# A side bank for transposes, hashes and sums, two banks for the down product, and preparing steps between the gated groups

## The chip, the core and the metric

The kernel runs on one core of one Trainium2 chip. The metric is the device time of one execution in microseconds (us). The program uses TensorE (PE) for matmuls, VectorE (DVE), ScalarE (ACT), GpSimd (POOL) and SyncE (SP); the last two issue the DMAs. Matmul results land in PSUM, which has eight banks per partition.

## The reference

Two blocks follow each other. The first is an attention whose mask lets a query see only the keys with the same 6-bit hash; the second is a gated feed-forward block on its output.

```python
q_bits = (np.einsum('bhsd,dk->bhsk', q, proj) > 0)     # k_bits alike, 6 bits
mask = q_bucket[:, :, :, None] == k_bucket[:, :, None, :]
scores = np.where(mask, scale * np.matmul(q, k.transpose(0, 1, 3, 2)), -1000000000.0)
attn = np.exp(scores - np.max(scores, axis=-1, keepdims=True))
attn = attn / (np.sum(attn, axis=-1, keepdims=True) + 1e-09)
x = np.matmul(attn, v)        # (4, 8, 768, 64) -> tokens (3072, 512)
g = x @ w_gate                # (512, 1536)
out = (g * (1.0 / (1.0 + np.exp(-g))) * (x @ w_val)) @ w_out
```

All data are float32; the weights come as float64 and are narrowed on the chip.

## The kernel before

The work is cut into 16 pairs of heads (4 batches of 4 pairs), each pair into two halves of 384 queries, each half into 6 chunks of 128 keys. One chunk of one half of one pair is a unit; there are 192.

- `score(u)` makes the scores of a unit for both heads of the pair: a bfloat16 matmul of the hash bits, which puts unequal hashes far below, then the float32 matmul of q and k, into one of two double banks `sc`; ScalarE takes the exponential into a ring of four tiles `A`.
- `attend(u)` multiplies `A` with v into the bank `av`, and VectorE adds `A` to the accumulator `acc`. After the sixth chunk ScalarE copies `av` out.
- `norm(u)` sums `acc` over the partitions with a matmul with ones (`sum`). VectorE adds a small number, takes the reciprocal and writes the normalised half to `xT`.
- `front(n)` prepares a pair in eight steps: four transposes of q or k (`tps`, three 128x128 blocks each; ScalarE copies the result), then four hash matmuls (`hps`, followed on VectorE by a comparison that writes the bits `qb` or `kb`). The steps are run two per two units, while the pair before is worked on.
- `push_ffn(b)` gives 72 atoms for a finished batch: 48 groups of eight matmul instructions (`g` and `val`, alternately; ScalarE's Tanh and VectorE's product free their banks), then 24 parts of the down product, of which four in a row fill one tile `po`; ScalarE copies it to `o` and SP stores it.
- `narrow()` turns the float64 words of the weights into float32 on VectorE, seven operations for each of 36 pieces. The pieces come over POOL's DMA queue.

A float32 matmul of the program is two matmul instructions in the profile. All engines run their own program in the order in which this code issues it. Nothing reorders it, so the order of calls in the loops at the end decides. The first batch has no atoms beside it ("alone"): there the loop takes one unit at a time: score, one step, attend of the unit before, one or two operations of `narrow`. From the second batch on (the gated part) it takes two units at a time: attend of the two units before, score of two units, two steps, then 3.1 atoms on average. When the units are used up, the atoms of the last batch follow by themselves.

PSUM: `sc` two double banks, `av` one, `po` one, and two banks `mm` that transposes, hashes, sums, gate and value groups share in turn. An instruction that wants a bank waits until the reader of its last content has ended.

Of the kernel before, what the change touches and what calls it, by code (L numbers as in the profile page):

```python
# [8 lines left out]
FP32 = mybir.dt.float32  # L9
BF16 = mybir.dt.bfloat16  # L10
I32 = mybir.dt.int32
ALU = mybir.AluOpType
AF = mybir.ActivationFunctionType
# [4 lines left out]
def kernel(  # L18
# [43 lines left out]
    wraw = ctx.enter_context(tc.tile_pool(name="wraw", bufs=2))  # L62
    sc_ps = ctx.enter_context(tc.tile_pool(name="sc_ps", bufs=2, space=PSUM))
    av_ps = ctx.enter_context(tc.tile_pool(name="av_ps", bufs=1, space=PSUM))
    po_ps = ctx.enter_context(tc.tile_pool(name="po_ps", bufs=1, space=PSUM))
    mm_ps = ctx.enter_context(tc.tile_pool(name="mm_ps", bufs=2, space=PSUM))

    ctx.enter_context(tc.manual_schedule())

    def bank(name):  # L70
        return mm_ps.tile([P, 512], FP32, tag="mm", name=name)


    pairs = [(b, pr) for b in range(B) for pr in range(NP)]
# [2 lines left out]
    def load(n):  # L77
        b, pr = pairs[n]
        for name, src in (("q", q), ("k", k)):
            t = raw.tile([P, NCH, 2, D], FP32, tag=name + "raw", name=name + "raw")  # L80
            for h in range(2):
                nc.sync.dma_start(t[:, :, h, :],
                                  src[b, 2 * pr + h].rearrange("(p c) d -> p c d", c=NCH))
            raws[name, n] = t
        t = raw.tile([P, 2, NCH, D], FP32, tag="vraw", name="vraw")
        nc.sync.dma_start(
            t.rearrange("p h c d -> p h (c d)"),
            v[b, 2 * pr : 2 * pr + 2].rearrange("h (p c) d -> p h (c d)", c=NCH),
        )
        raws["v", n] = t  # L90
# [11 lines left out]
            for at in (0, NBITS) if name == "q" else (0,):  # L102
                nc.sync.dma_start(hash_w[name][o : o + D, o + at : o + at + NBITS], proj[:, :])

    def column(name, first, second):
        t = konst.tile([P, 1], FP32, tag=name, name=name)
        nc.vector.memset(t, 0.0)
        for o in (0, D):
            nc.vector.memset(t[o : o + 2 * NBITS], second)
            nc.vector.memset(t[o : o + NBITS], first)  # L110
        return t

    less_q = column("less_q", 0.5, 0.0)
    above_k = column("above_k", 0.0, -1.0)
    times_k = column("times_k", 2.0 * OFF, -OFF)
    ident = konst.tile([P, P], FP32, tag="ident", name="ident")
    make_identity(nc, ident)
    ones = konst.tile([P, D], FP32, tag="ones", name="ones")
# [61 lines left out]
    def narrow_on(n):  # L180
        for _ in range(n):
            next(narrowing, None)
# [5 lines left out]
    T = {}  # L188
    bits = {}

    def front(n):


        def transpose(name, half):
            if half == 0:
                T[name, n] = opnd.tile([P, S], FP32, tag=name + "T", name=name + "T")
                bits[name, n] = opnd.tile([P, S], BF16, tag=name + "b", name=name + "b")
            ps = bank("tps")
            for i in range(CH):
                nc.tensor.transpose(ps[:, i * P : (i + 1) * P],  # L200
                                    raws[name, n][:, half * CH + i, :, :].rearrange("p h d -> p (h d)"),
                                    ident)
            nc.scalar.copy(T[name, n][:, half * HQ : (half + 1) * HQ], ps[:, 0:HQ])

        def hash_bits(name, half):
            cols = slice(half * HQ, (half + 1) * HQ)
            ps = bank("hps")
            nc.tensor.matmul(ps[:, 0:HQ], hash_w[name], T[name, n][:, cols], start=True, stop=True)  # L208
            o = bits[name, n][:, cols]
            if name == "q":  # L210
                nc.vector.tensor_scalar(o, ps[:, 0:HQ], scalar1=0.0, scalar2=less_q,  # L211
                                        op0=ALU.is_gt, op1=ALU.subtract)
            else:
                nc.vector.tensor_scalar(o, ps[:, 0:HQ], scalar1=above_k, scalar2=times_k,
                                        op0=ALU.is_gt, op1=ALU.mult)

        steps = []
        for half in range(2):
            for name in "qk":
                steps.append(lambda name=name, half=half: transpose(name, half))  # L220
        for half in range(2):
            for name in "qk":
                steps.append(lambda name=name, half=half: hash_bits(name, half))
        return steps
# [19 lines left out]
    def attend(u):  # L244
        n, half, c = units[u]
        a = ring[u % RING]
        if c == 0:
            av[n, half] = av_ps.tile([P, 512], FP32, tag="av", name="av")
        ps = av[n, half]
        for h in range(2):  # L250
            nc.tensor.matmul(ps[h * D : (h + 1) * D, 0:AW], raws["v", n][:, h, c, :], a[:, h, :],  # L251
                             start=c == 0, stop=c == NCH - 1)
        if c == 1:
            acc[n, half] = att.tile([P, 2, HQ], FP32, tag="acc", name="acc")
            nc.vector.tensor_tensor(acc[n, half], ring[(u - 1) % RING][:, :, 0:HQ],  # L255
                                    a[:, :, 0:HQ], op=ALU.add)
        elif c > 1:
            nc.vector.tensor_tensor(acc[n, half], acc[n, half], a[:, :, 0:HQ], op=ALU.add)  # L258
        if c == NCH - 1:
            av[n, half] = att.tile([P, AW], FP32, tag="avs", name="avs", bufs=1)  # L260
            nc.scalar.copy(av[n, half], ps[:, 0:AW])  # L261

    def norm(u):
        n, half, _ = units[u]
        b, pr = pairs[n]
        if pr == 0 and half == 0:
            xT[b] = xp.tile([P, NP, S], FP32, tag="xT", name="xT")
        ps = bank("sum")
        t = acc.pop((n, half))
        for h in range(2):  # L270
            nc.tensor.matmul(ps[h * D : (h + 1) * D, 0:HQ], ones, t[:, h, :], start=True, stop=True)  # L271
        a = av.pop((n, half))
        r = att.tile([P, HQ], FP32, tag="r", name="r", bufs=1)
        nc.vector.tensor_scalar(r, ps[:, 0:HQ], scalar1=S * EPS, scalar2=None, op0=ALU.add)  # L274
        nc.vector.reciprocal(r, r)  # L275
        e = att.tile([P, 1], FP32, tag="e", name="e")
        nc.vector.tensor_scalar(e, a[:, HQ : HQ + 1], scalar1=EPS, scalar2=None, op0=ALU.mult)
        nc.vector.scalar_tensor_tensor(out=xT[b][:, pr, half * HQ : (half + 1) * HQ],  # L278
                                       in0=a[:, 0:HQ], scalar=e, in1=r,
                                       op0=ALU.add, op1=ALU.mult)  # L280
        if pr == NP - 1 and half == 1:
            push_ffn(b)
# [4 lines left out]
    def push_ffn(b):  # L287
# [22 lines left out]

        def down(half, i, fs):
            if fs[0] == 0:
                now["o"] = po_ps.tile([P, DM], FP32, tag="po", name="po")
            ps = now["o"]
            for f in fs:
                nc.tensor.matmul(ps, hs[half][f][:, i * P : (i + 1) * P], wo[:, f, :],  # L316
                                 start=f == 0, stop=f == NF - 1)
            if fs[-1] == NF - 1:
                o = ffn.tile([P, DM], FP32, tag="o", name="o")
                nc.scalar.copy(o, ps)  # L320
                rows = out[b * S : (b + 1) * S, :].rearrange("(p c) m -> p c m", c=NCH)
                nc.sync.dma_start(rows[:, half * CH + i, :], o)
# [10 lines left out]

    for step in front(0):
        step()
    N = len(units)
    per = 2 * NCH
    steps = []  # L340
    due = []

    def prepare(u):
        n, at = divmod(u, per)
        if at == 0 and n + 1 < len(pairs):
            steps.extend(front(n + 1))
        if at == per - 2 and n + 2 < len(pairs):
            load(n + 2)

    def finish(u):  # L350
        while due:
            norm(due.pop(0))
        attend(u)
        if units[u][2] == NCH - 1:
            due.append(u)

    alone = NP * per
    for u in range(alone):
        prepare(u)
        score(u)  # L360
        if u % per >= 2 and steps:
            steps.pop(0)()
        if u > 0:
            finish(u - 1)
        narrow_on(2 if u % 6 == 3 else 1)

    rate = 3.1
    credit = 0.0
    left = [alone - 1]
    for u in range(alone, N + 2, 2):  # L370
        while left:
            finish(left.pop(0))
        if u >= N:
            while due:
                norm(due.pop(0))
            break
        prepare(u)
        score(u)
        score(u + 1)
        left = [u, u + 1]  # L380
        for _ in range(2):
            if u % per >= 2 and steps:
                steps.pop(0)()
        credit = credit + rate if atoms else 0.0
        while atoms and credit >= 1.0:
            credit -= 1.0
            atoms.pop(0)()
            narrow_on(4)
    for atom in atoms:
        atom()  # L390

# [31 lines left out]
```

## Time and profile before

| | |
|---|---|
| median of 3 runs | 1227.14 us (1227.07 to 1228.08) |
| profiled execution | 1227.17 us |
| its span | 1225.4 us |
| granted clock, mean | 0.997 |
| PE busy | 1174.4 us (96%) |
| VectorE busy | 540.5 us (44%) |
| ScalarE busy | 257.7 us (21%) |
| first score, first gate group | 13.50 us, 131.84 us |

PE is the engine that is nearly always busy, but a matmul's end in the profile is modelled, so that successive matmuls overlap a little. What one thing costs is read from the distance of two starts. In the first 340 us VectorE is busy too, since it narrows the weights there.

### The profile page before, as it was taken

Reading aid. Unit: us, or ns where it says so; the run is one execution under the profiler, and the core shown is the slowest. Engines: PE = TensorE matmul, PEld = TensorE weight load, DVE = VectorE, ACT = ScalarE, POOL = GpSimd, SP = SyncE. Lnnn points to the kernel's source line nnn. Section 1 sums busy time; section 2 is a strip of 40 time slices with the busy share of each in tenths; the row PEclk is TensorE's granted clock in tenths of the full one; section 3 lists DMA queues with packets and bytes.
Section 4 is the critical chain, followed back from the end, with each engine's and each line's share of the span. In section 5 each row is a group of like instructions: output and inputs, shape, how many; then the busy total and the mean of one; then the engine's idle time right before and its main releaser. Section 6 shows DMA issues by size and latency. Waiting matters only on the chain.

```text
span 1225.4 us, 10930 instructions
## 1 busy us (share of the span) xinstructions
PE 1174.4 (96%) x4480; PEld 569.4 (46%) x4480; DVE 540.5 (44%) x814; ACT 257.7 (21%) x409; POOL 19.3 (2%) x44
## 2 busy tenths in 40 slices
PE   8999989989899999999999999999999999999998
PEld 3333445445444444545553444554544334555533
DVE  4999788888832324234440333434234222222100
ACT  3444212212112122121221213222121111000000
POOL 0000000000000000000000000000000000000000
PEclk9999999999999999999999999999999999999999
DMA  6222314223200110100002012010000000000000
GB/s 155 74 74 74 91 52 124 68 70 108 69 22 18 43 48 1 39 1 1 13 1 56 18 34 48 1 39 1 14 1 1 18 18 17 1 1 0 1 26 26
DMA packets 63698, 44.76 MB, mean 37 GB/s; under 512 B 51872, under 2 KB 55968, under 8 KB 63648
## 3 DMA queue, kind: packets, MB, share of 16 engines
q1 hardware_dynamic: 58752, 26.23, 8.3%
q0 software_dynamic: 4896, 17.83, 4.6%
q8 instruction: 35, 0.57, 0.2%
q14 instruction: 15, 0.12, 0.0%
HBM read 37.76 MB, written 6.29 MB: 36 GB/s over the span
## 4 chain that ended last, share of the span: by engine, by line
PE 82%; DVE 12%; ACT 4%; issue 1%; DMA 0%; SPq 0%; ACTq 0%
PE po L316 21%; PE g L295 20%; PE val L295 19%; PE sc L240 9%; PE av L251 8%; DVE r L275 3%; ACT A L242 2%; DVE acc L258 2%; PE hps L208 2%; PE sum L271 2%; PE tps L200 1%; DVE qb L211 1%; DVE acc L255 1%; ACT o L320 1%; DVE xT L278 1%
## 5 line engine op out<-in xcount | busy, mean ns | idle before, releaser
L295 PE MATMUL val<-xT,wv 128*128 128x384 f32 x768 | 266.0, 489 | 15.9 <-DVE qb L211 10.9
L295 PE MATMUL g<-xT,wg 128*128 128x384 f32 x768 | 268.4, 493 | 12.5 <-DVE qb L211 7.8
L316 PE MATMUL po<-wo,ht 128*128 128x512 f32 x576 | 256.9, 597 | 9.8 <-ACT o L320 9.8
L242 ACT ACTIVATE A<-sc 128x768 f32<-128x768 f32 x192 | 155.6, 812 | 283.3 <-PE sc L240 256.8
L295 PEld LDWEIGHTS val<-xT,wv 128*128 128x128 f32 x768 | 144.2, 190 | 122.6 <-DVE qb L211 16.7
L295 PEld LDWEIGHTS g<-xT,wg 128*128 128x128 f32 x768 | 145.1, 191 | 119.7 <-DVE qb L211 12.9
L316 PEld LDWEIGHTS po<-wo,ht 128*128 128x128 f32 x576 | 106.7, 190 | 149.8 <-issue 126.4
L240 PE MATMUL sc<-qT,kT 64*128 64x384 f32 x768 | 155.1, 482 | 0.0
L258 DVE TENSOR_TENSOR acc<-acc,A 128x768 f32<-128x768 f32 x128 | 122.2, 954 | 66.8 <-ACT A L242 63.5
L302 DVE SCALAR_TENSOR_TENSOR t<-t,g 128x384 f32<-128x384 f32 x96 | 53.1, 554 | 222.9 <-ACT t L301 222.8
L251 PE MATMUL av<-A,vraw 128*64 128x386 f32 x768 | 149.4, 499 | 0.3 <-ACT A L242 0.2
L301 ACT ACTIVATE t<-g 128x384 f32<-128x384 f32 x96 | 47.0, 490 | 437.3 <-PE g L295 425.4
L307 DVE SCALAR_TENSOR_TENSOR ht<-t,val 128x384 f32<-128x384 f32 x96 | 53.1, 553 | 142.2 <-PE val L295 142.2
L251 PEld LDWEIGHTS av<-A,vraw 128*64 128x64 f32 x768 | 47.2, 136 | 83.9 <-issue 82.7
L275 DVE RECIPROCAL r<-r 128x384 f32<-128x384 f32 x32 | 81.7, 2553 | 1.1
L240 PEld LDWEIGHTS sc<-qT,kT 64*128 64x128 f32 x768 | 68.9, 189 | 16.4 <-issue 16.4
L274 DVE TENSOR_SCALAR r<-sum 128x384 f32<-128x384 f32 x32 | 17.7, 554 | 123.4 <-PE sum L271 122.9
L240 PE MATMUL sc<-qb,kb 64*128 64x384 bf16 x384 | 63.8, 329 | 0.0
L240 PEld LDWEIGHTS <-kb 64*128 64x128 bf16 x384 | 18.5, 93 | 81.2 <-issue 70.9
L320 ACT COPY o<-po 128x512 f32<-128x512 f32 x24 | 14.0, 585 | 155.4 <-PE po L316 148.4
L211 DVE TENSOR_SCALAR qb<-hps,less_q 128x384 bf16<-128x384 f32 x32 | 19.6, 614 | 45.0 <-PE hps L208 45.0
L261 ACT COPY avs<-av 128x386 f32<-128x386 f32 x32 | 15.4, 482 | 82.3 <-PE av L251 82.3
(56 smaller groups left out, 443.4 us busy)
## 6 DMA issues: line engine op xcount, KB each, us to landing
qraw<-in_q_dram SPq DMA_DIRECT2D x32, 192.0 KB, 4.4
kraw<-in_k_dram SPq DMA_DIRECT2D x32, 192.0 KB, 5.1
vraw<-in_v_dram SPq DMA_DIRECT2D x16, 384.0 KB, 3.5
words<-in_moe_w_val_dram POOLq DMA_DIRECT2D x12, 512.0 KB, 3.8
words<-in_moe_w_out_dram POOLq DMA_DIRECT2D x12, 512.0 KB, 3.6
out_dram<-o SPq DMA_DIRECT2D x24, 256.0 KB, 2.0
words<-in_moe_w_gate_dram POOLq DMA_DIRECT2D x10, 512.0 KB, 3.9
words<-in_moe_w_gate_dram SPq DMA_DIRECT2D x2, 512.0 KB, 6.1
```

The source lines that it names most:

```text
L211: nc.vector.tensor_scalar(o, ps[:, 0:HQ], scalar1=0.0, scalar2=less_q, op0=ALU.is_gt, op1=ALU.subtract)
L240: nc.tensor.matmul(sc[:, h, 0:HQ], x["k", n][rows, ks], x["q", n][rows, qs], start=start, stop=not start)
L242: nc.scalar.activation(ring[u % RING][:, :, 0:HQ], sc[:, :, 0:HQ], AF.Exp, scale=SCALE)
L251: nc.tensor.matmul(ps[h * D : (h + 1) * D, 0:AW], raws["v", n][:, h, c, :], a[:, h, :], start=c == 0, stop=c == NCH - 1)
L258: nc.vector.tensor_tensor(acc[n, half], acc[n, half], a[:, :, 0:HQ], op=ALU.add)
L275: nc.vector.reciprocal(r, r)
L295: nc.tensor.matmul(ps[:, 0:HQ], w[:, j, f * P : (f + 1) * P], x[:, j, half * HQ : (half + 1) * HQ], start=j == 0, stop=j == NJ - 1)
L301: nc.scalar.activation(t, ps[:, 0:HQ], AF.Tanh, scale=0.5)
L302: nc.vector.scalar_tensor_tensor(out=t, in0=t, scalar=1.0, in1=ps[:, 0:HQ], op0=ALU.add, op1=ALU.mult)
L307: nc.vector.scalar_tensor_tensor(out=ht, in0=now["t"], scalar=0.5, in1=ps[:, 0:HQ], op0=ALU.mult, op1=ALU.mult)
L316: nc.tensor.matmul(ps, hs[half][f][:, i * P : (i + 1) * P], wo[:, f, :], start=f == 0, stop=f == NF - 1)
L320: nc.scalar.copy(o, ps)
```

## The change

- Transposes, hashes and sums leave the two banks `mm` and get one bank of their own (`side_bank`), the one that the down product had. Only the first pair's steps, ahead of the loop, still use `mm`.
- The down product takes its tiles from the two banks `mm` in turn.
- The first batch is worked on two units at a time too, by the same loop as the rest.
- In an iteration the scores of two units now come first, then the sum that is due, then the attends of the two units before, then the atoms; the two steps are run after the first and the second atom. Without atoms, they run one right after the other, followed by two or three operations of `narrow`.
- The bits of q are made by ScalarE as a sign (Sign with a bias column), and the columns for k change their scale to match.
- VectorE's addition ahead of the reciprocal goes: the small number is added in the first addition of `acc`, and the reciprocal reads PSUM itself.

The diff, cut to its core:

```diff
+    aux_ps = ctx.enter_context(tc.tile_pool(name="aux_ps", bufs=1, space=PSUM))
...
+    def side_bank(name):
+        return aux_ps.tile([P, 512], FP32, tag="aux", name=name)
...
-    def front(n):
+    def front(n, bank=side_bank):
...
             if name == "q":
-                nc.vector.tensor_scalar(o, ps[:, 0:HQ], scalar1=0.0, scalar2=less_q,
-                                        op0=ALU.is_gt, op1=ALU.subtract)
+                nc.scalar.activation(o, ps[:, 0:HQ], AF.Sign, bias=nudge)
...
-            nc.vector.tensor_tensor(acc[n, half], ring[(u - 1) % RING][:, :, 0:HQ],
-                                    a[:, :, 0:HQ], op=ALU.add)
+            nc.vector.scalar_tensor_tensor(out=acc[n, half], in0=ring[(u - 1) % RING][:, :, 0:HQ],
+                                           scalar=S * EPS / P, in1=a[:, :, 0:HQ],
+                                           op0=ALU.add, op1=ALU.add)
...
-        ps = bank("sum")
+        ps = side_bank("sum")
...
-        nc.vector.tensor_scalar(r, ps[:, 0:HQ], scalar1=S * EPS, scalar2=None, op0=ALU.add)
-        nc.vector.reciprocal(r, r)
+        nc.vector.reciprocal(r, ps[:, 0:HQ])
...
-                now["o"] = po_ps.tile([P, DM], FP32, tag="po", name="po")
+                now["o"] = bank("po")
...
+    for u in range(0, N + 2, 2):
         n, at = divmod(u, per)
+        if u < N:
+            if at == 0 and n + 1 < len(pairs):
+                steps.extend(front(n + 1))
+            if at == per - 2 and n + 2 < len(pairs):
+                load(n + 2)
+            score(u)
+            score(u + 1)
         while due:
             norm(due.pop(0))
+        for x in left:
+            attend(x)
+            if units[x][2] == NCH - 1:
+                due.append(x)
         left = [u, u + 1]
+        mine = [steps.pop(0) for _ in range(2) if u % per >= 2 and steps]
+        if not atoms:
+            credit = 0.0
+            for step in mine:
+                step()
+            narrow_on(3 if u % 12 == 6 else 2)
+            continue
+        credit += rate
         while atoms and credit >= 1.0:
             credit -= 1.0
             atoms.pop(0)()
             narrow_on(4)
+            if mine:
+                mine.pop(0)()
```

Three places show what this does to the order on the engines. `tps<-ident,qraw` is a transpose of q, `hps<-qT,hashq` the hash matmul of q, `sc` a score, `av` an attend, `sum` the sum.

PE in the first batch, at the end of the first half of a pair, before:

```order
L240 MATMUL sc<-qT,kT 128x384 x2
L208 MATMUL hps<-kT,hashk 128x384
L271 MATMUL sum<-acc,ones 64x384 x2
L251 MATMUL av<-A,vraw 64x386 x2
L240 LDWEIGHTS kb
L240 MATMUL sc<-qb,kb 128x384
L240 LDWEIGHTS kb
L240 MATMUL sc<-qb,kb 128x384
L240 MATMUL sc<-qT,kT 128x384 x2
L208 MATMUL hps<-qT,hashq 128x384
```

and after:

```order
L244 MATMUL sc<-qT,kT 128x384 x2
L276 MATMUL sum<-acc,ones 64x384 x2
L255 MATMUL av<-A,vraw 64x386 x4
L213 MATMUL hps<-qT,hashq 128x384
L213 MATMUL hps<-kT,hashk 128x384
L244 LDWEIGHTS kb
```

Between the sum and the next hash there was an attend and a whole unit of scores; now two attends stand there, and the two hashes follow each other.

PE in a gated iteration with hashes, before:

```order
L240 MATMUL sc<-qT,kT 128x384 x2
L208 MATMUL hps<-qT,hashq 128x384
L208 MATMUL hps<-kT,hashk 128x384
L295 MATMUL val<-xT,wv 128x384 x4
L295 MATMUL g<-xT,wg 128x384 x4
L295 MATMUL val<-xT,wv 128x384 x4
L251 MATMUL av<-A,vraw 64x386 x4
```

and after:

```order
L244 MATMUL sc<-qT,kT 128x384 x2
L276 MATMUL sum<-acc,ones 64x384 x2
L255 MATMUL av<-A,vraw 64x386 x4
L299 MATMUL val<-xT,wv 128x384 x4
L213 MATMUL hps<-qT,hashq 128x384
L299 MATMUL g<-xT,wg 128x384 x4
L213 MATMUL hps<-kT,hashk 128x384
L299 MATMUL val<-xT,wv 128x384 x4
```

The hashes stood in a row ahead of the groups; now each has a group ahead of it and one behind it, and the attends stand behind the scores.

VectorE at a sum of the first batch, before:

```order
L214 TENSOR_SCALAR kb<-hps,above_k,times_k 128x384
L274 TENSOR_SCALAR r<-sum 128x384
L275 RECIPROCAL r<-r 128x384
L277 TENSOR_SCALAR e<-avs 128x1
L278 SCALAR_TENSOR_TENSOR xT<-avs,e,r 128x384
L160 SCALAR_TENSOR_TENSOR wg<-words,wg 128x512
L211 TENSOR_SCALAR qb<-hps,less_q 128x384
```

and after:

```order
L279 RECIPROCAL r<-sum 128x384
L281 TENSOR_SCALAR e<-avs 128x1
L282 SCALAR_TENSOR_TENSOR xT<-avs,e,r 128x384
L259 SCALAR_TENSOR_TENSOR acc<-A 128x768
L218 TENSOR_SCALAR kb<-hps,above_k,times_k 128x384
```

The bank of the sum was free after the short addition; now the reciprocal is its reader. The comparison for q is gone from this queue.

## Rows read from the trace of the kernel before

**Rows 1.** Page, part 1: busy time and share of the span, instructions.

```profile
PE 1174.4 (96%) x4480; PEld 569.4 (46%) x4480; DVE 540.5 (44%) x814; ACT 257.7 (21%) x409; POOL 19.3 (2%) x44
```

**Rows 2.** PE's waits over the run: who for whom; us in total, times, longest us.

```profile
PE val L295 <- DVE qb L211: 10.9, 6, 3.4
PE po L316 <- ACT o L320: 9.8, 14, 0.7
PE g L295 <- DVE qb L211: 7.8, 5, 3.5
...
PE val L295 <- ACT qT L203: 4.8, 9, 0.5
PE g L295 <- ACT qT L203: 4.5, 9, 0.5
```

**Rows 3.** Timeline, gated transposes in two stretches: start us, us, engine, line, operation, count, [idle].

```profile
457.81 1.52 PE L251 MATMUL av<-A,vraw 128*64 128x386 f32 x8
...
459.26 0.34 PE L240 MATMUL sc<-qb,kb 64*128 64x384 bf16 x2
...
460.98 0.55 PE L200 MATMUL tps<-ident,qraw 128*128 128x128 f32 x3
...
461.37 0.49 PE L200 MATMUL tps<-ident,kraw 128*128 128x128 f32 x3
...
461.87 0.47 ACT L203 COPY qT<-tps 128x384 f32<-128x384 f32 x1
...
462.40 2.85 PE L295 MATMUL val<-xT,wv 128*128 128x384 f32 x8 [0.54 <-ACT qT L203]
...
371.81 0.49 PE L200 MATMUL tps<-ident,kraw 128*128 128x128 f32 x3
372.14 2.74 PE L316 MATMUL po<-wo,ht 128*128 128x512 f32 x6
```

**Rows 4.** Timeline, two hash matmuls in a gated iteration.

```profile
486.88 0.91 PE L208 MATMUL hps<-qT,hashq 128*128 128x384 f32 x2
...
487.63 0.81 PE L208 MATMUL hps<-kT,hashk 128*128 128x384 f32 x2
```

**Rows 5.** Timeline, two long waits; then windows: busy us by engine, PEclk, DMA share.

```profile
253.36 2.85 PE L295 MATMUL val<-xT,wv 128*128 128x384 f32 x8 [3.40 <-DVE qb L211]
...
334.76 5.49 PE L295 MATMUL g<-xT,wg 128*128 128x384 f32 x8 [3.52 <-DVE qb L211]
...
250.00:300.00 50.00, 46.11 (x180) 24.66 (x182) 44.00 (x76) 9.03 (x15) 3.79 (x7) 1.00 0.29 88
300.00:350.00 50.00, 44.50 (x170) 22.22 (x167) 37.85 (x64) 9.68 (x15) 2.21 (x4) 0.93 0.15 53
```

**Rows 6.** Timeline, two tiles of the last down product.

```profile
1199.94 10.57 PE L316 MATMUL po<-wo,ht 128*128 128x512 f32 x24 [0.72 <-ACT o L320]
...
1211.23 10.57 PE L316 MATMUL po<-wo,ht 128*128 128x512 f32 x24 [0.72 <-ACT o L320]
```

**Rows 7.** Chain that ended last: start us, us, what; a down tile nobody stops.

```profile
640.66 10.30 PE po L316 x24
```

**Rows 8.** Page, part 5: costliest groups.

```profile
L301 ACT ACTIVATE t<-g 128x384 f32<-128x384 f32 x96 | 47.0, 490 | 437.3 <-PE g L295 425.4
...
L211 DVE TENSOR_SCALAR qb<-hps,less_q 128x384 bf16<-128x384 f32 x32 | 19.6, 614 | 45.0 <-PE hps L208 45.0
```

**Rows 9.** Timeline, first batch: first score, two sums, a reciprocal, first gate group.

```profile
13.50 0.34 PE L240 MATMUL sc<-qb,kb 64*128 64x384 bf16 x2
...
42.77 0.87 PE L271 MATMUL sum<-acc,ones 128*64 128x384 f32 x4 [0.77 <-DVE acc L258]
...
44.27 2.55 DVE L275 RECIPROCAL r<-r 128x384 f32<-128x384 f32 x1
...
70.74 0.87 PE L271 MATMUL sum<-acc,ones 128*64 128x384 f32 x4 [0.78 <-DVE acc L258]
...
131.84 2.85 PE L295 MATMUL g<-xT,wg 128*128 128x384 f32 x8 [0.48 <-ACT qT L203]
```

More of the change, by code (lines that the diff above doesn't have):

```diff
@@ L64 @@
     av_ps = ctx.enter_context(tc.tile_pool(name="av_ps", bufs=1, space=PSUM))
-    po_ps = ctx.enter_context(tc.tile_pool(name="po_ps", bufs=1, space=PSUM))
+    aux_ps = ctx.enter_context(tc.tile_pool(name="aux_ps", bufs=1, space=PSUM))
     mm_ps = ctx.enter_context(tc.tile_pool(name="mm_ps", bufs=2, space=PSUM))
@@ L103, with column @@
                 nc.sync.dma_start(hash_w[name][o : o + D, o + at : o + at + NBITS], proj[:, :])
-    def column(name, first, second):
+    def column(name, first, second, third, rest):
         t = konst.tile([P, 1], FP32, tag=name, name=name)
-        nc.vector.memset(t, 0.0)
+        nc.vector.memset(t, rest)
         for o in (0, D):
+            nc.vector.memset(t[o : o + 2 * NBITS + 1], third)
             nc.vector.memset(t[o : o + 2 * NBITS], second)
@@ L111, in column @@
         return t
-    less_q = column("less_q", 0.5, 0.0)
-    above_k = column("above_k", 0.0, -1.0)
-    times_k = column("times_k", 2.0 * OFF, -OFF)
+    nudge = column("nudge", -1e-37, -1e-37, 1.0, -1e-37)
+    above_k = column("above_k", 0.0, -1.0, -1.0, 0.0)
+    times_k = column("times_k", OFF, -OFF / 2, -NBITS * OFF / 2, 0.0)
     ident = konst.tile([P, P], FP32, tag="ident", name="ident")
@@ L331, in push_ffn @@
                     atoms.append(lambda half=half, i=i, f=f: down(half, i, range(f, f + 3)))
-    for step in front(0):
+    for step in front(0, bank):
         step()
@@ L339 @@
     per = 2 * NCH
+    rate = 3.1
+    credit = 0.0
     steps = []
+    left = []
     due = []
-    def prepare(u):
+    for u in range(0, N + 2, 2):
         n, at = divmod(u, per)
[L345 to L350, printed above, removed]
+        if u < N:
[5 more added lines that the diff above has]
+            score(u + 1)
         while due:
             norm(due.pop(0))
[L353 to L379, printed above, removed]
-        left = [u, u + 1]
[L381 to L384, printed above, removed]
+        for x in left:
+            attend(x)
+            if units[x][2] == NCH - 1:
+                due.append(x)
+        left = [u, u + 1]
+        mine = [steps.pop(0) for _ in range(2) if u % per >= 2 and steps]
+        if not atoms:
+            credit = 0.0
+            for step in mine:
[3 more added lines that the diff above has]
+        credit += rate
         while atoms and credit >= 1.0:
@@ L388 @@
             narrow_on(4)
+            if mine:
+                mine.pop(0)()
+        for step in mine:
+            step()
+    while due:
+        norm(due.pop(0))
     for atom in atoms:
```

## The prediction

> **What bounds the kernel now.** I read the page's busy shares first: PE is busy 1174.4 of 1225.4 us [rows 1], so a gain is either less PE work or less waiting. The matmuls stay the same in number and shape; what can go is waiting and changes of order. Then the waits of PE [rows 2]: five lines hold 37.8 us, of three kinds. PE waits for a bank that VectorE frees after a hash (7.8 + 10.9 us, 11 times), for a bank that ScalarE frees after a transpose (4.5 + 4.8 us, 18 times), for the one bank of the down product (9.8 us, 14 times). Then the timeline around one wait of each kind, because "idle" counts from a modelled end: the spacing of starts is the whole cost.
>
> **Down product, two banks: -13.3 us.** A tile of 24 matmuls takes 10.30 us when nothing stops it [rows 7]; where it must wait for the copy, the next tile starts 11.29 us after it (1199.94 to 1211.23 [rows 6]). That is 0.99 us; some waits stand beside a change of array shape that costs up to 0.1 anyway, so I take 0.95, 14 times [rows 2]. With two banks in turn, the copy has a whole tile's time. The gate and value groups share these two banks, but a batch's down product begins only after its last value group. Nothing new is late here.
>
> **Steps between gated groups: -12.6 and -23.1 us.** Before, two transposes run back to back and the next gate or value group needs the bank that the first has filled: the second transpose starts at 461.37 and the group at 462.40, 1.03 us, where a transpose of the same shape that nobody holds up needs 0.33 (371.81 to 372.14) [rows 3]. 0.7 us, 18 times: 12.6. For hashes the same wait is for VectorE: 18.7 us of idle in 11 waits [rows 2], and in each the drain that the modelled end adds, 0.16 us (a transpose's 0.49 less its 0.33 [rows 3]): 20.5. In one place more was lost: after a 3.52 us wait a gate group took 5.49 us in place of 2.85, in a stretch whose granted clock was 0.93 [rows 5]: 2.6. After the change a step lies behind a group and ahead of another, on its own bank, and the next step comes one group (2.6 us or more) later. Its copy or Sign takes about 0.5 us [rows 3, 8], so the bank is free by then. The Sign is not in the trace: lower bound the 0.47 us copy of the same shape, upper the 0.61 of the VectorE form it replaces; I take 0.49, the Tanh's mean, the nearest in engine and shape [rows 8]. 32 of them, 16 us more on an engine busy 257.7 us [rows 1], nothing on the path. The program has one table load before and after.
>
> The sum's bank is now held until the reciprocal ends. In a gated iteration: sum starts 1.73 us after the first score (two scores take 1.72 [rows 3]), ends 0.87 later, reciprocal 2.55 [rows 9]: free at about 5.2. Two attends and one group end at 1.73 + 0.70 + 1.45 + 2.68 = 6.55, and only then does a step want the bank. 1.3 us of slack, so no wait, unless VectorE starts the reciprocal late. That can happen where the weights are narrowed: VectorE is busy 44.0 of 50 us there [rows 5]. It loses 32 hash comparisons (0.61 us each [rows 8]) and 32 additions ahead of the reciprocal; the first addition of each accumulator gets a third operand (I estimate from nothing up to 0.3 us, 32 times). I count 1 us for this stretch; the bounds are 0 and all that hashes cost today, 23.
>
> Sequence changes on PE: before, an iteration goes groups, attends, scores, steps; now groups, scores, attends. There are three changes of array shape in both. The one that the rows show costs 0.06 us at the first transpose (0.39 against 0.33 [rows 3]), the others I estimate at up to three times that; I take the balance as 0, within 2 us either way.
>
> **First batch in twos, one side bank: +10.7 us.** This stretch has no groups between steps, and I work it out by itself. Before, one pair of heads takes 27.97 us (sum to sum, 42.77 to 70.74), with a 0.77 us wait at each of these two sums [rows 9]. After, a pair is six iterations of two scores and two attends, 3.17 us bare (457.81 to 460.98 [rows 3]). Two have no step: 3.17 each. The four others issue two steps with nothing between and a single bank:
> - two transposes: 0.1 for the extra change of shape, then from the first to the second 0.55 modelled, 0.05 to ScalarE, 0.47 copy, 0.06 back [rows 3] = 1.13, then 0.4 for the second: 4.8.
> - two hashes: 3.17 + 0.1, then 0.91 [rows 4] + 0.05 + 0.49 + 0.06 = 1.5, then 0.85: 5.6.
> - transposes in the iteration with a sum: they wait for the reciprocal, 1.73 + 0.87 + 2.55 + 0.1 = 5.25, then 1.13 + 0.43: 6.8.
> - hashes in the iteration with the other sum: 5.25 + 1.5 + 0.85: 7.6.
>
> Together 2 x 3.17 + 4.8 + 5.6 + 6.8 + 7.6 = 31.1, so 3.2 more per pair, though the twos have halved the changes of shape and the sum no longer waits. The first pair has no early sum and starts with scores only: 31.1 - 2.0 - 1.3 = 27.8. From the first score (13.50 [rows 9]) to the first gate group: 27.8 + 3 x 31.1 + 3.17 + 3.87 = 128.1, so 141.6 to 141.9, against 131.84 [rows 9]: +10. By then before has done two transposes that now follow: +0.65. What is queued behind these waits is PE's whole stream; ScalarE's and VectorE's exponentials and additions just come later. VectorE loses two additions and two comparisons per pair here, and PE waited for it only at sums. SP's reload of v waits for attends up to one unit later, a whole pair before it is needed. Narrowing is 54 operations done instead of 56 when the first group is issued, and the first value group follows 4 more: enough. Bounds: if both waits were hidden, the stretch would gain 12 us (16 x 0.83 + 7 x 1.4 = 23 less); if every copy and reciprocal also stood behind a 0.81 us exponential, 16 x 0.8 = 13 us worse.
>
> **The sum.** 1225.4 - 13.3 - 12.6 - 23.1 + 10.7 + 1 = 1188.1 us of span; 1.8 us lie around it (1227.17 less 1225.4), and the profiled execution agrees with the median of 1227.14. **1190 us.**
>
> **Rivals.**
> (a) The first batch loses nothing: the side bank comes free sooner, because the reciprocal reads a bank as soon as the first half of a sum is in, or the copies are quicker. Against it: both steps need one bank and the copies and the reciprocal have their rows. Half of the 23 us hidden gives about 1179.
> (b) The hash waits come back as waits for VectorE elsewhere, on the gate and value banks or through a late reciprocal, in the stretch where it narrows. For it: 44.0 of 50 us busy. Against: each group frees its bank half a microsecond after VectorE reaches it, and PE needs it a group later. All of the 23.1: 1213; half: 1201.
> (c) Slower than before: the first batch falls to half clock. Its waits, 1.4 and 0.8 us in each iteration of some 6, could make TensorE look idle; its roughly 95 us of matmuls would double, to about 1285. The whole gain of 37 us is gone once 37 us of matmul work runs at 1.2 GHz. Against: a wait of 3.40 us left the granted clock at 1.00 [rows 5], and only the 3.52 us one was followed by a slow group.
> The Trainium skill ("TensorE: Matmul & The Clock Gate", section "A second HAM failure mode: psum-queue depth-cycling") says that short idles of PE between groups of matmuls that cycle through PSUM banks can make the clock swing between its two levels. By that rule (c) would hold; no run here has shown it after waits of 1.4 us.
> (d) That it doesn't do what it says: the down product has two banks to itself, so at least 13.3 us are nearly sure; for no change all else would have to cancel.
>
> **How the numbers follow.** The forecast has 0.68, (a) 0.15, (b) 0.12, (c) 0.03, no change 0.02. The forecast's own spread is 1183 to 1197. The range reaches half into (a) and to the middle of (b), 1176 to 1206; outside lie about 0.05 of (a), 0.06 of (b), (c), (d) and a few hundredths of the forecast. This kernel's measurement can tell 0.2% from no change, 2.5 us. Faster 0.95, same 0.02, slower 0.03.
>
> **What would show it.** PE's waits for o should vanish from the list, and those of gate and value groups for qT and qb. New lines should stand there: a transpose waiting for qT's copy and a hash waiting for qb's Sign (16 pairs, near 0.5 us idle each), and a transpose or hash waiting for the reciprocal (7 times, over 1 us). The first gate group should start near 142 us. The clock should show 1.00 near 334. I am wrong if the first gate group starts before 132, if gate and value groups still wait in the narrowing stretch, or if the first batch shows a clock under 0.9.

## The result and the profile after

The changed kernel takes 1187.62 us (median of 4 runs, 1186.9 to 1187.78) against 1227.61 us before (4 runs). The ratio is 0.9673, 95% interval 0.9656 to 0.969: faster by 3.3%. 1190 had been forecast. The profiled execution took 1187.64 us with a span of 1185.9.

PE's waits over the whole run, in the columns of [rows 2]:

```profile
PE hps L213 <- DVE e L281: 5.5, 4, 1.4
PE hps L213 <- ACT qb L216: 5.4, 8, 0.7
PE tps L205 <- DMA qraw<-in_q_dram: 4.8, 1, 4.8
PE tps L205 <- ACT qT L208: 4.6, 8, 0.6
PE tps L205 <- DVE e L281: 4.1, 3, 1.4
PE tps L205 <- DMA kraw<-in_k_dram: 1.0, 1, 1.0
```

All five lines of [rows 2] are gone: no gate, value or down group waits for anything. Apart from the two DMA lines of the start, four lines are left, and all of them are steps waiting for the side bank, in the first batch: 16 times for the copy or the Sign of the step before, 7 times for VectorE at a sum. ("DVE e" is the small operation behind the reciprocal in the queue; the reciprocal's end releases the bank.)

The page's busy shares, and the groups of the two operations that were new to the trace or had a new source (columns as in [rows 1] and [rows 8]):

```profile
PE 1156.9 (98%) x4480; PEld 573.2 (48%) x4480; DVE 508.2 (43%) x756; ACT 280.3 (24%) x441; POOL 19.2 (2%) x44
...
L279 DVE RECIPROCAL r<-sum 128x384 f32<-128x384 f32 x32 | 81.8, 2556 | 151.9 <-PE sum L276 151.9
...
L216 ACT ACTIVATE qb<-hps,nudge 128x384 bf16<-128x384 f32 x32 | 18.6, 581 | 69.4 <-PE hps L213 69.3
```

The reciprocal takes 2556 ns out of PSUM, as long as out of SBUF before (2.55 us, [rows 9]). The Sign takes 581 ns, near the upper of the two bounds that were given for it, not 490.

One iteration of the first batch with a sum, all engines (timeline; answers to [rows 9]):

```profile
46.69 1.47 PE L255 MATMUL av<-A,vraw 128*64 128x386 f32 x8
...
46.91 2.56 DVE L279 RECIPROCAL r<-sum 128x384 f32<-128x384 f32 x1 [1.39 <-PE sum L276]
...
49.52 0.55 PE L205 MATMUL tps<-ident,qraw 128*128 128x128 f32 x3 [1.36 <-DVE e L281]
...
50.11 0.48 ACT L208 COPY qT<-tps 128x384 f32<-128x384 f32 x1 [3.18 <-PE tps L205]
...
50.64 0.55 PE L205 MATMUL tps<-ident,kraw 128*128 128x128 f32 x3 [0.57 <-ACT qT L208]
```

The two attends end near 48.2. The transpose of q starts at 49.52, when the reciprocal has left the bank, and that of k 1.12 us later, when the copy has: the two waits of the prediction, at the size it gave (1.13 us from start to start).

PE in a gated iteration with hashes, in the stretch in which VectorE narrows the weights (timeline, PE alone; answers to [rows 4, 5]):

```profile
167.14 2.85 PE L299 MATMUL g<-xT,wg 128*128 128x384 f32 x8
169.83 0.81 PE L213 MATMUL hps<-qT,hashq 128*128 128x384 f32 x2
170.47 2.74 PE L299 MATMUL val<-xT,wv 128*128 128x384 f32 x8
173.05 0.81 PE L213 MATMUL hps<-kT,hashk 128*128 128x384 f32 x2
173.70 1.78 PE L299 MATMUL g<-xT,wg 128*128 128x384 f32 x5
```

A hash costs 0.64 us between two groups and the next group starts at once. And the last down product, where [rows 6] had a wait in each tile, is one line:

```profile
1159.77 22.48 PE L320 MATMUL po<-wo,ht 128*128 128x512 f32 x52
```

So the time went two ways. From the first gate group to the end of the span the kernel before needed 1225.4 - 131.84 = 1093.6 us, the changed one 1185.9 - 143.37 = 1042.5: 51.0 less. From the first score to the first gate group it needed 118.3 us and now needs 130.1 (13.25 to 143.37): 11.8 more.

### The profile page after: what moved, and what is told of

The parts are those of the page before. It is cut to its first block, busy times and chain, and to the rows that moved or that the text cites. A ratio compares the mean times of both kernels' runs of the same rounds, so it can differ in the third digit from the quotient of the medians.

```text
span 1185.9 us, 10899 instructions
## 1 busy us (share of the span) xinstructions
PE 1156.9 (98%) x4480; PEld 573.2 (48%) x4480; DVE 508.2 (43%) x756; ACT 280.3 (24%) x441; POOL 19.2 (2%) x44
## 4 chain that ended last, share of the span: by engine, by line
PE 97%; DVE 2%; ACT 1%; DMA 0%; SPq 0%; issue 0%; ACTq 0%
PE val L299 21%; PE g L299 21%; PE po L320 21%; PE sc L244 14%; PE av L255 11%; PE hps L213 4%; PE sum L276 2%; PE tps L205 2%; DVE r L279 2%; ACT qb L216 0%; ACT qT L208 0%; DMA kraw<-in_k_dram 0%; SPq L85 0%; ACT A L246 0%; ACT o L324 0%
## 5 line engine op out<-in xcount | busy, mean ns | idle before, releaser
L299 PEld LDWEIGHTS g<-xT,wg 128*128 128x128 f32 x768 | 142.5, 190 | 105.1 <-DVE acc L263 6.0
L279 DVE RECIPROCAL r<-sum 128x384 f32<-128x384 f32 x32 | 81.8, 2556 | 151.9 <-PE sum L276 151.9
L255 PE MATMUL av<-A,vraw 128*64 128x386 f32 x768 | 144.8, 498 | 0.0
L255 PEld LDWEIGHTS av<-A,vraw 128*64 128x64 f32 x768 | 49.6, 137 | 82.4 <-issue 81.3
L218 DVE TENSOR_SCALAR kb<-hps,above_k,times_k 128x384 bf16<-128x384 f32 x32 | 21.6, 675 | 83.9 <-PE hps L213 83.4
L216 ACT ACTIVATE qb<-hps,nudge 128x384 bf16<-128x384 f32 x32 | 18.6, 581 | 69.4 <-PE hps L213 69.3
L213 PE MATMUL hps<-qT,hashq 128*128 128x384 f32 x64 | 27.7, 515 | 5.5 <-DVE e L281 5.5
```

Source lines behind the costliest of these rows:

```text
L279: nc.vector.reciprocal(r, ps[:, 0:HQ])
L299: nc.tensor.matmul(ps[:, 0:HQ], w[:, j, f * P : (f + 1) * P], x[:, j, half * HQ : (half + 1) * HQ], start=j == 0, stop=j == NJ - 1)
```

## Experiments

The kernels of this section ran on three chips, on which the kernel before took 1230.0 to 1230.5 us (medians), against 1227.61 beside the result. Differences below are to the changed kernel's 1187.62, so they run across chips; the ratios are to the kernel before on the same chip. That the chips can be compared shows in the gated part: from the first gate group to the last sum, the kernels that change nothing there took 851.9 to 852.2 us, and the changed kernel 852.2. One thing belongs to no experiment: the changed kernel's profile has a spell at half clock in the first batch that cost it some 1.5 us (shown further down). The kernels with the add ahead of the reciprocal, with two banks, and with the first batch in ones have none, and owe that much of their gain to it.

### The reader of the sum's bank

```diff
-        nc.vector.reciprocal(r, ps[:, 0:HQ])
+        nc.vector.tensor_scalar(r, ps[:, 0:HQ], scalar1=0.0, scalar2=None, op0=ALU.add)
+        nc.vector.reciprocal(r, r)
```

> The changed kernel with VectorE's short addition put back ahead of the reciprocal (it adds zero here), so that the side bank's reader is the addition (about 0.55 us) and no longer the reciprocal (2.56 us); everything else as changed. Theory (the hold of the side bank by the reciprocal is what the first batch waits for, 7 waits of about 1.4 us): the bank is free about 0.6 us after the sum, before the two attends end, so the 7 waits vanish and the first gate group starts near 133 us instead of 143.4; time 1187.6 - 10 = 1177 to 1179 us. Rival (VectorE's queue, not the bank's reader, sets those waits; 32 more additions only lengthen it): 1187 to 1190 us, and the 7 waits stay over 1 us.

Measured: 1176.15 us (ratio 0.9561, 0.9547 to 0.9576), 11.5 less than the changed kernel. First gate group at 131.93. The same place as above in its timeline, at a sum:

```profile
45.73 0.56 DVE L279 TENSOR_SCALAR r<-sum 128x384 f32<-128x384 f32 x1
...
46.32 2.55 DVE L280 RECIPROCAL r<-r 128x384 f32<-128x384 f32 x1
...
46.91 0.55 PE L205 MATMUL tps<-ident,qraw 128*128 128x128 f32 x3
```

The transpose starts in the middle of the reciprocal and has no wait beside it; the seven waits are gone from the list, at the price of 32 operations of 0.56 us on VectorE that nobody waits for. About 1.5 of the 11.5 us is the spell at half clock, which the expectation had not counted; the time lies just below its range. The hold of the bank was the cause of the seven waits. The part of the change that takes an operation away was a loss here.

### Two banks for the steps of the first batch

```diff
-                steps.extend(front(n + 1))
+                steps.extend(front(n + 1, bank if n < NP else side_bank))
```

> The changed kernel, but the steps of the first batch take the two banks that gate and value groups use later (idle in that stretch); sums stay on the side bank, and from the second batch on all is as changed. Theory (in the first batch the single side bank costs 16 waits for the copy or the Sign, 0.8 to 0.94 us each, and 7 for the reciprocal, 1.43 us each): all of it goes, 16 x 0.87 + 7 x 1.43 = 24 us, first gate group near 119 to 121 us, time 1163 to 1167 us. Rival (VectorE or ScalarE take over as the bound in that stretch: VectorE was busy 45 of 50 us there in the kernel before): only half of it, 1173 to 1178 us, with PE waiting for the exponentials or for the accumulators.

Measured: 1162.44 us (1162.02 to 1162.75; ratio 0.9448, 0.9432 to 0.9463), 25.2 less than the changed kernel. First gate group at 118.51, so the stretch from the first score takes 105.1 us. PE and the reciprocal in the timeline, at the same place:

```profile
41.99 1.47 PE L255 MATMUL av<-A,vraw 128*64 128x386 f32 x8
...
42.21 2.56 DVE L279 RECIPROCAL r<-sum 128x384 f32<-128x384 f32 x1
43.39 0.55 PE L205 MATMUL tps<-ident,qraw 128*128 128x128 f32 x3
43.77 0.49 PE L205 MATMUL tps<-ident,kraw 128*128 128x128 f32 x3
...
44.20 0.34 PE L244 MATMUL sc<-qb,kb 64*128 64x384 bf16 x2
```

Two transposes and the scores follow each other without a gap, with the sum's bank held by the reciprocal until 44.77. Neither VectorE nor ScalarE takes over, though VectorE is busy 47.0 of 50 us between 50 and 100 us (window, columns as in [rows 5]):

```profile
50.00:100.00 50.00, 49.79 (x298) 21.98 (x298) 47.00 (x63) 26.64 (x41) 2.12 (x4) 1.00 0.32 86
```

This one-line change beats both kernels: of all that were run it is the fastest. It needs nothing but banks that lay idle in that stretch.

### The first batch in ones

The first experiment undoes the twos in the changed kernel, the second in the kernel with two banks just shown, where no order waits for the side bank.

```diff
-    for u in range(0, N + 2, 2):
+    alone = NP * per
+    for u in range(alone):
...
+        score(u)
+        if at >= 2 and steps:
+            steps.pop(0)()
+        if u > 0:
...
+            attend(u - 1)
...
+        narrow_on(2 if u % 6 == 3 else 1)
+    left = [alone - 1]
+    for u in range(alone, N + 2, 2):
```

> The changed kernel with the first batch one unit at a time, as in the kernel before; all the rest as changed. Theory (in twos the batch saves some 8.5 us of changes of array shape and 3 us of waits at sums, and pays 24 us at the side bank; in ones the steps lie 2 us apart, so that the waits for the copies go and only some 1.1 us of each wait for the reciprocal stays): a pair takes 29.5 to 30.5 us instead of 31.2, time 1182 to 1186 us. Rival (the order in twos is a gain by itself in this kernel): 1190 us or more.

> The kernel whose first batch's steps take two banks (1162.4 us), with the first batch one unit at a time instead of two; so neither order waits for the side bank there, and the difference is what taking two units at a time is worth by itself. Theory (twos halve the changes of array shape, 8.5 us over the batch, and put two scores ahead of the sum, which then no longer waits for its accumulator, 3 us in four waits): 1162.4 + 11.5 = 1173 to 1175 us, first stretch 116 to 117.5 us against 105.1. Rival (twos were only of use because of the banks): 1162 to 1165 us.

Measured: 1182.51 us (ratio 0.9612, 0.9598 to 0.9626) and 1171.05 us (ratio 0.9523, 0.9495 to 0.955). With the single bank, ones are 5.1 us faster than twos, of which 1.5 is the spell at half clock; with two banks, ones are 8.6 us slower than twos (first stretch 113.5 us against 105.1). Apart from the start, neither kernel with two banks has more than 0.2 us of waits of PE for another engine, so the second figure is what the order of PE's own work is worth, as the halved changes of array shape had been put at (8.5 us, from the spacings of starts). It is less than the 10.6 to 12.6 us expected: the 3 us of waits at the sum did not come. So the twos were a gain that the single bank more than took back.

### The bits of q on VectorE again

```diff
-                nc.scalar.activation(o, ps[:, 0:HQ], AF.Sign, bias=nudge)
+                nc.vector.tensor_scalar(o, ps[:, 0:HQ], scalar1=0.0, scalar2=less_q,
+                                        op0=ALU.is_gt, op1=ALU.subtract)
```

> The changed kernel with the bits of q made by VectorE's comparison again instead of ScalarE's Sign; banks and order as changed. Theory (the place between the groups takes away most of the hash waits; the Sign only matters where VectorE's queue is long): where the weights are narrowed the second hash may wait for VectorE up to 1 to 3 us in some 6 iterations, and in the first batch four hashes wait some 1.5 us more; elsewhere nothing: 1192 to 1204 us. Rival A (the Sign is what took the hash waits away): all of the 23 us come back, 1209 us or more. Rival B (the Sign does nothing): 1186.5 to 1189 us.

Measured: 1197.34 us (ratio 0.9733, 0.9713 to 0.9752), 9.7 more. From the first gate group to the last sum it took 857.9 us where the changed kernel took 852.2, so 5.8 of it are gated. The rest is in the first batch, and 1.5 of that is no wait: the clock fell twice there, once more than in the changed kernel. All five gated waits lie in the narrowing stretch, before 346 us; one of them (timeline):

```profile
174.45 2.74 PE L300 MATMUL val<-xT,wv 128*128 128x384 f32 x8
...
176.90 0.69 DVE L174 CUSTOM_DVE_ANT_0 wg<-words,wg 128x1024 uint16<-128x1024 uint16 x1
177.51 0.61 DVE L216 TENSOR_SCALAR qb<-hps,less_q 128x384 bf16<-128x384 f32 x1
...
178.18 0.91 PE L213 MATMUL hps<-kT,hashk 128*128 128x384 f32 x2 [0.99 <-DVE qb L216]
```

The comparison stands behind four narrowing operations, and a whole group does not cover that. Later in the run, where nothing is narrowed, the group covers it.

### The Sign alone, in the kernel before

```diff
-                nc.vector.tensor_scalar(o, ps[:, 0:HQ], scalar1=0.0, scalar2=less_q,
-                                        op0=ALU.is_gt, op1=ALU.subtract)
+                nc.scalar.activation(o, ps[:, 0:HQ], AF.Sign, bias=nudge)
```

> The kernel before with one part of the change alone: the bits of q as signs by ScalarE. Theory (the group behind the hashes waits for the reader of the first hash's bank, and the Sign is quick; the second bank, read by VectorE, is needed a group later): most of the 11 waits for VectorE shrink to a wait of about 0.7 us for the Sign, 23.1 - 11 x 0.7 = 15 us: 1210 to 1215 us. Rival (the wait moves to the comparison for k, which stands behind the reciprocal in VectorE's queue): 1222 to 1228 us.

Measured: 1206.2 us (ratio 0.9812, 0.9791 to 0.9832), so 21 to 24 us less than the kernel before (span 1204.6 against 1225.4; 1206.2 against 1229.97 on the same chip, where the kernel before mostly showed a lower mean clock, 0.994 or 0.995, than in its profile), more than either theory gave it. By the two spans it is 20.8 us: from the first gate group to the last sum it took 876.8 us against 895.8, so 19.0 are gated, some 2.8 of them the spell at half clock of [rows 5]; 2.1 are in the first batch, where sums wait less for the accumulator. The waits for qT and for o stay as in [rows 2] and those for qb are gone. In their place stand three short ones for the comparison of k, the rival's mechanism at a small size:

```profile
PE g L296 <- DVE kb L215: 0.9, 2, 0.6
PE val L296 <- DVE kb L215: 0.7, 1, 0.7
```

Why the Sign costs nearly nothing even with no group between shows in its timeline:

```profile
471.44 0.81 PE L210 MATMUL hps<-kT,hashk 128*128 128x384 f32 x2
471.64 0.58 ACT L213 ACTIVATE qb<-hps,nudge 128x384 bf16<-128x384 f32 x1
472.28 2.85 PE L296 MATMUL val<-xT,wv 128*128 128x384 f32 x8
```

The first hash's Sign runs beside the second hash, which takes 0.64 us anyway; the group starts 0.84 us after it, a wait of 0.2 us and not the 0.7 that I had put down. The comparison takes 0.61 us [rows 8], hardly more than the Sign's 0.58. What made PE wait before was VectorE's queue, not the work of the comparison.

### Steps ahead of the groups, on the side bank

```diff
+        for step in mine:
+            step()
         credit += rate
...
             narrow_on(4)
-            if mine:
-                mine.pop(0)()
-        for step in mine:
-            step()
```

> The changed kernel with the two steps of a gated iteration run one right after the other ahead of the groups, still on the one side bank; all the rest as changed. Theory (the place between the groups is what hides the single bank): the waits of the first batch now stand in every gated iteration with steps: 22 times two transposes 0.79 us, 22 times two hashes 0.94 us, 22 sums 1.5 us, 17 + 21 + 33 = 71 us: 1253 to 1265 us, slower than the kernel before. Rival (the side bank alone takes the waits away, since groups no longer share banks with steps): 1187 to 1195 us.

Measured: 1275.38 us (ratio 1.0374, 1.0351 to 1.0397), 87.8 more than the changed kernel and slower than the kernel before. First the waits of PE, then PE at one sum (timeline):

```profile
PE hps L213 <- DVE e L281: 22.9, 15, 2.4
PE tps L205 <- DVE e L281: 21.0, 14, 2.4
PE hps L213 <- ACT qb L216: 20.1, 30, 0.7
PE tps L205 <- ACT qT L208: 17.1, 30, 0.6
```

```profile
468.97 0.55 PE L205 MATMUL tps<-ident,qraw 128*128 128x128 f32 x3 [1.36 <-DVE e L281]
470.09 0.55 PE L205 MATMUL tps<-ident,kraw 128*128 128x128 f32 x3 [0.57 <-ACT qT L208]
470.47 3.79 PE L299 MATMUL g<-xT,wg 128*128 128x384 f32 x6
```

The window around it (columns as in [rows 5]):

```profile
450.00:500.00 50.00, 47.49 (x180) 23.53 (x182) 12.59 (x17) 11.05 (x18) 0.00 (x0) 0.97 0.18 43
```

The waits of the first batch stand in the gated iterations too: these four lines hold 81.1 us where the changed kernel has 19.6. That is 61.5 us more, or 72 with a drain of 0.16 us in each of the 66 further waits: the 71 us expected. What the forecast had left out, and why it was passed by 10 us, is the clock: the mean granted over this run is 0.985 against 0.999 (0.014 of 1274.5 us is 18 us), and the gate group above took 3.79 us for six instructions of its eight. So a side bank without a group between its users is worse than the old order.

### The last down product on one bank

```diff
-                now["o"] = bank("po")
+                now["o"] = (side_bank if b == B - 1 else bank)("po")
```

> The changed kernel with the down product of the last batch alone, which runs after the last unit, on the one side bank (idle by then); the other batches use two banks as changed. Theory (each tile then waits for the copy of the tile before, 0.88 + 0.1 us): 5 waits, +4.4 to 5.0 us, 1192 to 1192.7 us. Rival (the copy is hidden anyway by PE's queue): 1187 to 1188 us.

Measured: 1191.89 us (1191.48 to 1192.17; ratio 0.9696, 0.9679 to 0.9712), 4.3 more. Its first score came 0.9 us earlier than in the changed kernel's profile; from the start of the last sum to the last copy it took 191.7 us (994.60 to 1186.32) against 186.8 (995.55 to 1182.33), 4.9 more for five waits. Two tiles in a row:

```profile
1164.38 10.57 PE L320 MATMUL po<-wo,ht 128*128 128x512 f32 x24 [0.72 <-ACT o L324]
1175.67 4.56 PE L320 MATMUL po<-wo,ht 128*128 128x512 f32 x10 [0.72 <-ACT o L324]
```

11.29 us from start to start, as in [rows 6]. A wait costs 0.98 us (4.9 us for five), where the prediction took 0.95.

## Why the prediction was right, and where not

- **Down product, -13.3.** Right: the waits for o are gone, and undoing it for five tiles costs 4.3 to 4.9 us.
- **Steps between groups, -12.6 and -23.1.** The sum was right, one attribution was not. From the first gate group on 51.0 us went, where these terms with the down product give 49.0, less 1 for the narrowing stretch and 0.65 for the two transposes that come later: 47.4. Of the missing 3.6 us, 1 is the narrowing stretch, where no wait is left. The rest is mainly the changes of shape, whose balance I had set at 0 within 2. Summed from the distances of starts in both profiles, the hash waits were worth 20.5 us as forecast and the clock 2.8, the transposes' waits 11.6 (17 of the 18; the first one stands ahead of the first gate group [rows 9]) and those for o 12.1, a little less than forecast; the changes of shape gave 4.7. Most of that is at the steps: behind the scores the first hash took 0.91 us [rows 4] and the transposes of q 0.55 [rows 3], and between groups they take 0.81 and 0.49. But I gave all of the 23.1 us of hashes to the place between the groups and nothing to the Sign. The Sign alone, in the old order, takes back 19.0 gated us; the place alone, with VectorE's comparison, leaves 5.8 us in the gated part. Each of the two was nearly enough, so the sum was right while the cause it named was only one of two. The transposes have no such second remedy in this change: their waits stay when only the Sign is brought in. The new order with the steps still on the two shared banks was not run, so whether they needed the side bank as well is open.
- **The order is what makes the single bank free.** Shown: without it, 87.8 us more. The slack of 1.3 us between reciprocal and step was enough even where VectorE is busiest.
- **The first batch, +10.7.** Right in kind and in place: 16 waits and 7 waits, as counted, 12.5 and 10.7 us by the distances of starts, where 13 and 10 had been put down. A pair takes 31.2 us (sum to sum, 46.00 to 77.21) for the 31.1 worked out. The Sign's 0.58 us instead of 0.49 adds 0.1 to each pair of hashes. The stretch is 1.8 us longer than the 10 forecast. Most of that is one spell at half clock (below), worth 1.5 us; the prediction had it as a rival only. That 1190 came within 2.4 us is partly luck: the gated part gained 3.6 us more than forecast and the first batch lost 1.8 us more, and the two misses cancel in part.
- **Rival (a)**, first batch for nothing, was wrong for the kernel as it is. The 25.2 us that two banks bring confirm the bound of 23 us given for these waits, with the 1.5 us of clock on top.
- **Rival (b)**, hash waits that return at VectorE, did not happen; with the comparison back on VectorE a quarter of it does.
- **Rival (c)**, the clock, happened once, for 1.5 us, not for the stretch. PE's timeline and the windows:

```profile
111.95 0.55 PE L205 MATMUL tps<-ident,qraw 128*128 128x128 f32 x3 [1.37 <-DVE e L281]
113.06 0.55 PE L205 MATMUL tps<-ident,kraw 128*128 128x128 f32 x3 [0.57 <-ACT qT L208]
113.54 0.34 PE L244 MATMUL sc<-qb,kb 64*128 64x384 bf16 x2
113.72 0.99 PE L244 MATMUL sc<-qT,kT 64*128 64x384 f32 x4
114.50 0.53 PE L244 MATMUL sc<-qb,kb 64*128 64x384 bf16 x2
114.82 1.49 PE L244 MATMUL sc<-qT,kT 64*128 64x384 f32 x4
116.24 2.18 PE L255 MATMUL av<-A,vraw 128*64 128x386 f32 x8
```

```profile
100.00:150.00 50.00, 44.79 (x238) 19.51 (x237) 38.19 (x53) 20.24 (x30) 1.59 (x3) 0.97 0.28 69
300.00:350.00 50.00, 50.00 (x197) 24.56 (x195) 38.82 (x64) 12.68 (x20) 2.25 (x5) 1.00 0.16 53
```

A score that takes 0.81 us elsewhere takes 1.49 here, behind an iteration with both waits. The other six iterations of that kind show nothing. The 2.6 us of [rows 5] near 334 are gone, as forecast.

Other runs say more. Four kernels have iterations in which PE waits for the reciprocal and then for a copy or for bits: the changed one, the one with the last down product on one bank, the one with the comparison back on VectorE, and the one with the steps ahead of the groups. In their profiles the granted clock fell to its half level 1, 1, 2 and 11 times before the last matmul, each time in or right behind such an iteration; there are 50 of these, so 35 show no fall. In the first batch it is not the same iteration from run to run. With the last down product on one bank it came nearly 80 us earlier, behind hashes:

```profile
34.61 0.91 PE L213 MATMUL hps<-qT,hashq 128*128 128x384 f32 x2 [1.36 <-DVE e L281]
36.19 0.91 PE L213 MATMUL hps<-kT,hashk 128*128 128x384 f32 x2 [0.67 <-ACT qb L216]
...
37.33 1.49 PE L244 MATMUL sc<-qT,kT 64*128 64x384 f32 x4
```

The rule of the Trainium skill that stood beside (c) ("TensorE: Matmul & The Clock Gate", section "A second HAM failure mode: psum-queue depth-cycling") finds agreement in kind: the granted clock swings where PE waits often and briefly for a bank, most of all in the kernel with the steps ahead of the groups (0.985 over the run). Its mean stays at 1.000 in the five kernels without an iteration of that kind: with the add ahead of the reciprocal, with two banks in the first batch, with ones in the first batch (both kernels), and with the Sign alone. Short waits by themselves are not enough, then: with the Sign alone PE still waits 32 times for a copy, 0.5 to 0.7 us each.

## What to carry to other kernels

In this kernel a single bank was as good as two wherever more work than its reader needs lay between two of its users; count that work at each place where the users follow each other, and give them another bank where there is none. An instruction that is saved ahead of a slow reader of PSUM can cost more than it saves, as it did here, since the bank is then held for as long as the slow one runs. When a change brings two remedies for one wait, put only one of them into the sum, and try each alone before you call either the cause.

## What the runs showed of the hardware

- The granted clock can fall to half behind waits much shorter than the 3.52 us of [rows 5]: 15 times in 50 iterations that hold a wait of 1.36 to 2.4 us for the reciprocal and a shorter one of 0.57 us or more for a copy or for bits, while a wait of 3.40 us [rows 5] left it at 1.00, and so did single waits of 0.5 to 1.1 us (Sign alone; first batch in ones). One fall cost some 1.5 us. What decides is not settled by these runs.
- A Sign with a bias column that writes bfloat16 took 581 ns on ScalarE where a Tanh of the same shape took 490 [rows 8]. Whether the function, the column or the type makes the difference was not tried.
- VectorE's reciprocal of 128x384 took 2.55 us from SBUF and 2.56 from PSUM: where it reads from made no difference to its time, only to how long the bank is held.
